# A Strassen sum made by accumulating DMA transfers in place, and the buffer of another sum moved

## The chip, the cores and the metric

One core of one Trainium2 chip. The metric is the device time of one execution in microseconds (us), of the slowest core, which here is the only one.

Names of engines in the profile: PE is TensorE (matmuls), PEld its weight loads, DVE is VectorE, ACT is ScalarE, POOL is GpSimd, SP is SyncE.

## The reference, cut to what matters

```python
# x (8, 4096, 192) -> causal convolution with 7 taps, softmaxed weights per head -> (32768, 192)
h = x @ w_in                        # 192 -> 2048
g = h * np.clip(h + 3, 0, 6) / 6
out = g @ w_out                     # 2048 -> 192, all in float32
```

## The kernel before

The 32768 tokens go through in 32 blocks of 1024. Block 0 is direct; the other 31 use Strassen's scheme with seven products (the variant with sums S1 to S4) for both matrix products. In a block, PE first makes the hidden values (the *hidden phase*, four units of two slots), VectorE gates them into the tile `g`, and then PE makes the output products (the *output phase*). `g` has the quarters A11, A21, A12, A22; the output phase needs

- S1 = A21 + A22, used by product P5,
- S3 = A11 - A21, used by P7,
- S2 = S1 - A11, used by P6, and S4 = A12 - S2, used by P3.

S1 and S3 are made by POOL after every unit, S2 and S4 by VectorE in the output phase. S1 has a buffer of its own, S2, S3 and S4 lie over quarters that are no longer needed.

```python
S2, S3, S4 = A11, A21, A12
...
def h_phase(left):
    for u, plan in enumerate(PLANS):
        ...                                   # matmuls, relu, gates of unit u
        if u:
            g_sums(nc.gpsimd, (1, 3), range(2 * u - 2, 2 * u), 2)
...
forms = {
    1: (S1, A21, A22, ALU.add), 3: (S3, A11, A21, ALU.subtract),
    2: (S2, S1, A11, ALU.subtract), 4: (S4, A12, S2, ALU.subtract),
}
...
def out_strassen(i, conv):
    for u in conv: u()                        # VectorE: convolution of the next block
    b, bank = three(1, 2, 0)                  # PE: P1, a third of P2
    ...
    g_sums(nc.vector, (2,), every, 4)         # VectorE: S2, in two halves
    b, bank = three(4, 2, 1)
    ...
    swap(slice(0, K3))                        # DMA: halves of y change places
    b, bank = by_quarters(2, 2)
    ...
    g_sums(nc.vector, (4,), every, 4)         # VectorE: S4
    b7, bank7 = three(7, 5, 0)                # PE: P7 reads S3, P5 reads S1
    b, bank = three(6, 5, 1)                  # PE: P6 reads S2
    b, bank = three(3, 5, 2)                  # PE: P3 reads S4
```

## Time and profile before

2410.7 us median of 3 runs (2410.63 to 2410.88).

| engine | busy us | share of the span of 2409.1 us |
|---|---|---|
| PE | 2399.2 | 100% |
| DVE | 2088.8 | 87% |
| ACT | 1077.1 | 45% |
| POOL | 671.3 | 28% |
| DMA, 84.65 MB | | 17 to 18% of 16 engines |

How to read it: shares near 100% show candidates for a bound. Only the chain of work that ended last tells whether the others matter, and a block of the timeline tells how much idle time lies between a result and its first use.

### The profile page before, as it was taken

To read this page: it belongs to the slowest core of one execution; us is meant where nothing else is said; L and a number is where in the kernel's file an instruction comes from. 1 tells how busy PE (TensorE), PEld (TensorE's weight loads), DVE (VectorE), ACT (ScalarE), POOL (GpSimd) and SP (SyncE) were. 2 spreads that over 40 slices of the span, in tenths; PEclk is the share of its full clock that TensorE was granted. 3 is DMA by queue.
4 is the path that set the end of the run, shared out by engine and by line. 5 is a ranking of instruction groups with operands and counts; after the bars stand their busy time and mean duration, and the time that the engine had idled before them with its cause. 6 is when DMAs were issued, how large, how long until landed. Compare 5 with 4: busy or idle time off the path is not lost.

```text
span 2409.1 us, 40076 instructions
## 1 busy us (share of the span) xinstructions
PE 2399.2 (100%) x16468; PEld 1008.8 (42%) x16468; DVE 2088.8 (87%) x2534; ACT 1077.1 (45%) x1827; POOL 671.3 (28%) x280
## 2 busy tenths in 40 slices
PE   9999999999999999999999999999999999999998
PEld 4334444334444344443444434444334444344443
DVE  8788888988888888898888898888898888888896
ACT  7234553345543355433454334553335543355433
POOL 2423321233221333122332223322233312333122
PEclk9999999999999999999999999999999999999999
DMA  5211122101122011221112211122201122111210
GB/s 145 40 26 29 27 40 40 39 18 26 39 41 40 19 35 27 40 41 22 32 27 40 41 34 21 27 40 40 40 18 34 30 40 40 21 34 27 40 27 14
DMA packets 227336, 84.65 MB, mean 35 GB/s; under 512 B 205456, under 2 KB 210576, under 8 KB 227152
## 3 DMA queue, kind: packets, MB, share of 16 engines
q1 hardware_dynamic: 225848, 81.56, 17.1%
q8 instruction: 129, 2.11, 0.4%
q10 hardware_dynamic: 1208, 0.27, 0.1%
q14 instruction: 55, 0.45, 0.1%
q0 software_dynamic: 96, 0.26, 0.0%
HBM read 31.72 MB, written 25.17 MB: 24 GB/s over the span
## 4 chain that ended last, share of the span: by engine, by line
PE 99%; DVE 1%; DMA 0%; issue 0%; ACTq 0%; SPq 0%; DVEq 0%
PE psum L311 50%; PE psum L437 48%; DVE y L263 0%; DMA x<-in_x_dram 0%; DMA y<-y 0%; DVE c L541 0%; ACTq L92 0%; DVE scale L174 0%; DVE y L259 0%; DVE sig L199 0%; DVE scale L195 0%; DVE top L178 0%; DVE xt L547 0%; SPq L276 0%; DVEq L259 0%
## 5 line engine op out<-in xcount | busy, mean ns | idle before, releaser
L437 PE MATMUL psum<-g,w_out 128*32 128x512 f32 x9312 | 1163.6, 592 | 0.0
L311 PE MATMUL psum<-y,w_in 64*128 64x512 f32 x3664 | 885.1, 592 | 2.1 <-DVE y L263 1.9
L497 POOL TENSOR_TENSOR s<-g 128x1024 f32<-128x1024 f32 x124 | 293.5, 2367 | 1645.1 <-DVE g L321 1645.1
L317 ACT ACTIVATE r<-psum,half 128x512 f32<-128x512 f32 x1024 | 641.3, 688 | 241.3 <-PE psum L311 234.2
L437 PEld LDWEIGHTS psum<-g,w_out 128*32 128x32 f32 x9312 | 337.4, 110 | 811.7 <-issue 769.9
L321 DVE SCALAR_TENSOR_TENSOR g<-r,psum 128x512 f32<-128x512 f32 x1024 | 641.8, 681 | 4.8 <-ACT r L317 1.1
L437 PE MATMUL psum<-s,w_out 128*32 128x512 f32 x1488 | 638.5, 592 | 0.0
L311 PEld LDWEIGHTS psum<-y,w_in 64*128 64x128 f32 x3664 | 430.2, 187 | 378.7 <-issue 299.4
L311 PE MATMUL psum<-y,w_in_t 64*128 64x512 f32 x1984 | 523.8, 592 | 0.0
L403 DVE TENSOR_TENSOR psum<-psum,p 128x512 f32<-128x512 f32 x496 | 324.6, 694 | 196.0 <-PE psum L311 187.3
L263 DVE SCALAR_TENSOR_TENSOR y<-x,c_sb,y 128x1536 f32<-128x1536 f32 (+1 forms) x210 | 416.6, 1991 | 6.6
L533 ACT COPY c<-psum 32x512 f32<-32x512 f32 x188 | 108.7, 578 | 600.7 <-PE psum L437 599.9
L497 POOL TENSOR_TENSOR g<-g 128x1024 f32<-128x1024 f32 x124 | 338.0, 2725 | 9.7
L311 PEld LDWEIGHTS psum<-y,w_in_t 64*128 64x128 f32 x1984 | 247.1, 186 | 194.3 <-issue 124.9
L541 DVE TENSOR_TENSOR c<-c,psum 32x512 f32<-32x512 f32 (+1 forms) x187 | 128.1, 685 | 81.8 <-ACT c L533 75.8
L396 ACT COPY psum<-psum 128x512 f32<-128x512 f32 x248 | 138.9, 571 | 72.6 <-PE psum L311 57.4
L437 PEld LDWEIGHTS psum<-s,w_out 128*32 128x32 f32 x1488 | 162.4, 110 | 1.2 <-issue 1.2
L399 ACT COPY p<-psum 128x512 f32<-128x512 f32 x248 | 133.2, 591 | 40.7 <-PE psum L311 40.0
L497 DVE TENSOR_TENSOR g<-s,g 128x2048 f32<-128x2048 f32 x62 | 139.3, 2287 | 3.9 <-POOL g L497 2.3
L497 DVE TENSOR_TENSOR g<-g 128x2048 f32<-128x2048 f32 x62 | 139.4, 2289 | 2.0 <-PE psum L437 1.0
L601 ACT COPY c<-psum 96x512 f32<-96x512 f32 x30 | 17.4, 581 | 174.5 <-PE psum L437 174.5
L606 ACT COPY c<-psum 96x512 f32<-96x512 f32 x30 | 17.4, 581 | 170.0 <-PE psum L437 170.0
(46 smaller groups left out, 431.9 us busy)
## 6 DMA issues: line engine op xcount, KB each, us to landing
out_dram<-xt SPq DMA_DIRECT2D x382, 64.0 KB, 2.0
y<-y SPq DMA_DIRECT2D x62, 384.0 KB, 4.8
x<-in_x_dram SPq DMA_DIRECT2D x55, 388.5 KB, 5.7
stage<-in_moe_w_in_dram SPq DMA_DIRECT2D x16, 192.0 KB, 4.4
stage<-in_moe_w_out_dram SPq DMA_DIRECT2D x8, 384.0 KB, 5.2
x<-in_x_dram SPq DMA_DIRECT2D x7, 384.0 KB
y<-y SPq DMA_DIRECT2D x6, 128.0 KB, 2.3
x<-in_x_dram SPq DMA_DIRECT2D x2, 128.0 KB, 4.4
```

The source lines that it names most:

```text
L263: nc.vector.scalar_tensor_tensor(out=to, in0=x[:, part, k + t : k + t + W], scalar=c, in1=to, op0=ALU.mult, op1=ALU.add,)
L311: nc.tensor.matmul(out=psum[:, b], lhsT=w[r], rhs=y[r, third_of_y], start=start, stop=stop, skip_group_check=onto,)
L317: nc.scalar.activation(r6, h, ACT.Relu, bias=half[:], scale=1.0 / 6.0)
L321: nc.vector.scalar_tensor_tensor(out=out, in0=r6, scalar=1.0, in1=h, op0=ALU.min, op1=ALU.mult)
L396: nc.scalar.copy(out=psum[:, bank["b"]], in_=psum[:, bank["a"]])
L399: nc.scalar.copy(out=self.p5[:], in_=psum[:, bank["e"]])
L403: nc.vector.tensor_tensor(out=psum[:, to], in0=psum[:, bank["b"]], in1=self.p5[:], op=ALU.add)
L437: lambda p=p: nc.tensor.matmul(out=bank[j * QS : (j + 1) * QS], lhsT=w_out[:, p, w, cols], rhs=x[:, p], start=(first and p == ps_[0]), sto ...
L497: engine.tensor_tensor(out=o[:, r], in0=a[:, r], in1=b[:, r], op=op)
L533: nc.scalar.copy(out=dst[rows(q)], in_=src[rows(j)])
L541: nc.vector.tensor_tensor(out=out, in0=x, in1=y, op=op)
L601: nc.scalar.copy(out=p1[:], in_=bank[m])
```

## The change

S1 is no longer computed by POOL into a buffer of its own. After each unit, POOL makes S3 alone, into that buffer, and then issues a DMA that adds A22 onto A21 in SBUF; A21 is then S1. The intent is to take about half of the elementwise work off POOL, and with it POOL's collisions with VectorE (in the kernel before, a convolution instruction beside S3 takes 3.81 us where the others take 1.82).

```diff
-    S2, S3, S4 = A11, A21, A12
+    S2, S1, S4 = A11, A21, A12
@@ h_phase
             if u:
-                g_sums(nc.gpsimd, (1, 3), range(2 * u - 2, 2 * u), 2)
+                slots = slice(2 * u - 2, 2 * u)
+                g_sums(nc.gpsimd, (3,), range(NP)[slots], 2)
+
+                nc.gpsimd.dma_start(
+                    out=S1[:, slots], in_=A22[:, slots], accum_op=ALU.add
+                )
@@ g_sums
-            1: (S1, A21, A22, ALU.add), 3: (S3, A11, A21, ALU.subtract),
+            3: (S3, A11, A21, ALU.subtract),
@@ products
-        5: (None, T1), 6: (S2, T2), 7: (S3, T3),
+        5: (S1, T1), 6: (S2, T2), 7: (None, T3),
...
-        return mm(bank, j, S1 if n == 5 else x, w, q, ks, True, True)
+        return mm(bank, j, S3 if n == 7 else x, w, q, ks, True, True)
@@ launch of the blocks
-        S1 = ss.tile([P, NP, N], F32, name="s1")[:]
+        S3 = ss.tile([P, NP, N], F32, name="s3")[:]
```

## The prediction

> **What bounds the kernel now.** I read the page first: the busy table, the slices, the chain of work that ended last. The columns of the first are busy time, share of the span, and instructions.
>
> ```profile
> span 2409.1 us, 40076 instructions
> PE 2399.2 (100%) x16468; PEld 1008.8 (42%) x16468; DVE 2088.8 (87%) x2534; ACT 1077.1 (45%) x1827; POOL 671.3 (28%) x280
> PEclk9999999999999999999999999999999999999999
> PE 99%; DVE 1%; DMA 0%; issue 0%; ACTq 0%; SPq 0%; DVEq 0%
> PE psum L311 50%; PE psum L437 48%; DVE y L263 0%; DMA x<-in_x_dram 0%; DMA y<-y 0%; DVE c L541 0%; ACTq L92 0%; DVE scale L174 0%; DVE y L259 0%; DVE sig L199 0%; DVE scale L195 0%; DVE top L178 0%; DVE xt L547 0%; SPq L276 0%; DVEq L259 0%
> ```
>
> The matmuls are busy for 2399.2 of 2409.1 us at full granted clock, and the chain is PE for 99%. A busy PE could still be a badly pipelined one, so I checked one repeat. The kernel has 31 equal blocks after the first; in the timeline one block runs from 322.96 to 397.22 us, 74.26 us, and has two parts: hidden-layer matmuls (L311, 38.1 us) and output matmuls (L437, 36.2 us). In the steady part of the output phase the timeline starts four quarter-width streams, 8 PE instructions, every 0.86 us, which is 107 ns each; 336 of them make 36.0 of the 36.2 us. No hole is left to win there.
>
> Then the part concerned, the sums of g (L497), by groups:
>
> ```profile
> L497 POOL TENSOR_TENSOR s<-g 128x1024 f32<-128x1024 f32 x124 | 293.5, 2367 | 1645.1 <-DVE g L321 1645.1
> L497 POOL TENSOR_TENSOR g<-g 128x1024 f32<-128x1024 f32 x124 | 338.0, 2725 | 9.7
> L497 DVE TENSOR_TENSOR g<-s,g 128x2048 f32<-128x2048 f32 x62 | 139.3, 2287 | 3.9 <-POOL g L497 2.3
> L263 DVE SCALAR_TENSOR_TENSOR y<-x,c_sb,y 128x1536 f32<-128x1536 f32 (+1 forms) x210 | 416.6, 1991 | 6.6
> ```
>
> The first is S1 on POOL, 124 = 31 blocks x 4 units of two slots. The second is S3, the third S2 on DVE, and the fourth the convolution of the next block, which DVE runs before S2. POOL waits 1645 us in all for the gates, so it is not a bound. Last the order of time in one block; columns are start, duration, engine and what.
>
> ```profile
> 356.37 2.36 POOL L497 TENSOR_TENSOR s<-g 128x1024 f32<-128x1024 f32 x1 [4.64 <-DVE g L321]
> 358.81 2.37 POOL L497 TENSOR_TENSOR g<-g 128x1024 f32<-128x1024 f32 x1
> 362.69 2.40 POOL L497 TENSOR_TENSOR s<-g 128x1024 f32<-128x1024 f32 x1 [1.51 <-DVE g L321]
> 365.17 3.78 POOL L497 TENSOR_TENSOR g<-g 128x1024 f32<-128x1024 f32 x1
> 363.06 1.81 DVE L259 TENSOR_SCALAR y<-x,c_sb 128x1536 f32<-128x1536 f32 x1
> 364.90 13.08 DVE L263 SCALAR_TENSOR_TENSOR y<-x,c_sb,y 128x1536 f32<-128x1536 f32 x6
> 377.89 4.49 DVE L497 TENSOR_TENSOR g<-s,g 128x2048 f32<-128x2048 f32 x2
> 361.04 16.08 PE L437 MATMUL psum<-g,w_out 128*32 128x512 f32 x147
> 376.53 0.59 PE L437 MATMUL psum<-s,w_out 128*32 128x512 f32 x1
> ```
>
> The last S1 is ready at 362.69 + 2.40 = 365.09 us. PE first reads S1 at 376.53, for the last unit three quarters of a 6.86 us group later, at 381.7. DVE starts S2, which reads S1, at 377.89, because it is behind the convolution and not because S1 is late. So the last S1 lies finished for 11 to 17 us. That slack is what the change spends.
>
> [...] The trace before has no accumulating DMA. Its nearest kin is the swap of y, from SBUF to SBUF: 384 KB, 4.8 us to landing; two of them moved 0.79 MB in about 4 us of DMA activity (379 to 383 us), some 200 GB/s[...]. I use the measured rate. [...] in the block shown the first three scalar_tensor_tensor of the convolution average 2482 ns, with S3 beside them, and the next four 1819 ns, with POOL idle; one takes 3.81 us, and S3 stretches from 2.37 to 3.78 us.
>
> **The change part by part.** It removes 124 POOL adds x 2.37 us = 293.5 us of POOL. S3 stays, but is now the first in each unit and writes the separate buffer. It adds 124 DMAs issued from POOL, each adding A22 to A21 over 128 partitions x 1024 f32 = 512 KB. The order of instructions shows that each waits for the S3 before it on POOL (S3 reads A21, which the DMA overwrites). P5 on PE waits for the DMA of each unit separately, S2 on DVE for two at a time.
>
> Duration of one, estimated: a plain copy of 512 KB at 200 GB/s is 2.6 us[...]. On the path: S3 takes the old place of S1, 337.5, 346.9, 356.4 and 362.7, so the DMAs start at 339.8, 349.3, 358.7 and 365.1. They are 9.5, 9.4 and 6.4 us apart, and don't pile up at 4 to 5 us of transfer each. The last lands at 371 to 373 us, before 376.5 and before S2. PE waits for nothing new: 0 us.
>
> Beside the path: DVE loses only the overlap of one POOL add in place of two. In before the loss is 3 x (2482 - 1819) = 2.0 us a block; S3 now ends at 365.1, as the first scalar_tensor_tensor begins (364.9), so nearly all comes back: about 30 x 2.0 = 60 us of DVE, with S2 starting near 376 us. DVE is 87% busy and off the chain, so it buys 0 us of time. The later S3 (3.78 us under contention) falls to 2.4 us. POOL falls from 671 to 671 - 293.5 - 124 x (2.725 - 2.37) = 333 us, the issues not counted.
>
> Buffers: A21 now holds S1, read till the last group of the block (ends at 397.1), where S3 was free one group after 376.5. Its next writers are gates on OTHER results of the next block, from about 330 us in the preceding block's terms, 7 us after the hidden phase began at 323; by then PE has long left the group. A12 holds S4 with the same lifetime already and nobody waits. S3's new buffer is read in one group only, so POOL is free earlier.
>
> Sum: 2410.7 + 0 from PE, with at most some tenths of a microsecond a block for waits that PE now does on DMA semaphores in place of POOL's (the number is the same, four and four). I say 2411.
>
> **The rivals.** (1) The accumulate is slow. If they run one after the other in T us, the last ends at 339.8 + 4T; it must be there by 381.7 us, so T up to 10.5 us (49 GB/s) is hidden. Above it the queue of four bites: T = 11.5 would delay P5 by 4 us a block, 31 x 4 = 124 us, 5%. For it: an addition inside a DMA is nowhere in this trace, and A21 is cut into 2 KB runs where the swap moves 6 KB runs. Against it: the threshold is under half the rate that I estimate. A lone last DMA may even take 16.6 us. (2) VectorE becomes the bound by the chain S2, pieces, S4: S2's second half must start by 390.25 (start of P3) - 2.29 - 2.13 - 2.29 = 383.5 us. That's a later deadline than P5's, so it needs the same slow DMA; 0 us otherwise. (3) The DMAs starve others: DMA share is 0.41 at 330 to 340 us (stores and x) and about 0 from 340 to 376, just where the four run, so they meet little. The swap comes at 378 after the last landing. If the landing slipped to 385, the swap would be slowed by some 3 us, and YS1 has till 397. (4) A gain: freeing POOL and 60 us of DVE might shorten the path. Against it: PE has no hole to fill; at most the 10 us in which PE is not busy, mostly the start that the change doesn't touch, and so never 2%. [...]
>
> **Range and chances.** If the step of zero is right the time moves within about 0.2%, as 31 blocks x 0.1 us is 3 us; that gives 2407 to 2416. I stretch the upper end to 2420 for a delay of 0.3 us a block. Slower by over 2% needs 48 us, 1.6 us a block, which only rival 1 or something unseen in the queue gives: 7%. Faster by over 2%: 1%, since PE alone is busy for 2399 us.
>
> **What would show it.** Right: PE still 2399 us busy and on 99% of the chain; POOL near 333 us; the convolution group down by about 60 us; landing of the new DMAs 6 to 8 us; no wait of PE for a DMA. Wrong: PE weight loads or matmuls that wait for the DMA on g, S2 on DVE idle before it until that DMA, landing above 12 us, or a hidden phase that waits on gates into A21.

The 4 to 5 us of transfer, and with it a landing after 6 to 8 us, are the estimate, above the 2.6 us of a plain copy at the swap's 200 GB/s: no trace before the result showed how long an accumulating DMA takes.

## The result

2410.67 us median of 4 runs (2410.61 to 2410.71), beside 2410.79 us for the kernel before (4 runs). The ratio is 1.0, 95% interval 0.9985 to 1.0014. Ratios here and below are the mean time of one kernel's fast runs over that of the other's of the same rounds, so not quite the ratio of the medians quoted.

The page of the changed kernel: span and busy times, the engines of the chain, four groups of instructions, and one line of the DMA issues (count, size of each, median us from issue to landing).

```profile
span 2408.9 us, 40142 instructions
PE 2399.1 (100%) x16468; PEld 1010.3 (42%) x16468; DVE 2028.6 (84%) x2534; ACT 1077.0 (45%) x1827; POOL 481.5 (20%) x280
...
PE 99%; DVE 1%; DMA 0%; issue 0%; ACTq 0%; DVEq 0%
...
L502 POOL TENSOR_TENSOR s<-g 128x1024 f32<-128x1024 f32 x124 | 292.5, 2359 | 1802.7 <-PE psum L311 1685.4
...
L263 DVE SCALAR_TENSOR_TENSOR y<-x,c_sb,y 128x1536 f32<-128x1536 f32 (+1 forms) x210 | 356.9, 1707 | 6.6
...
L502 DVE TENSOR_TENSOR g<-g 128x2048 f32<-128x2048 f32 x124 | 278.6, 2288 | 5.9 <-DMA g<-g 3.3
...
L431 POOL DMA_DIRECT2D g<-g x124 | 149.1, 1202 | 39.5 <-DVE g L321 27.5
...
g<-g POOLq DMA_DIRECT2D x124, 512.0 KB, 5.0
```

PE is as busy as before to 0.1 us, and still the chain. POOL fell by 189.8 us and VectorE by 60.2 us, 59.7 of it in the convolution (416.6 to 356.9 us), and none of it shows in the span. PE waits for none of the new DMAs; VectorE does so once, for 3.3 us. (In this trace POOL's line puts 1685 us of waiting down to PE, where before it named the gates. POOL's S3 is released by several semaphores, and the last one is inferred; it is the same long wait for the next block's hidden values.)

The timeline of the block that the prediction read, in the changed kernel (start, duration, engine, what):

```profile
362.55 2.38 POOL L502 TENSOR_TENSOR s<-g 128x1024 f32<-128x1024 f32 x1 [2.47 <-issue]
365.23 1.20 POOL L431 DMA_DIRECT2D g<-g  x1 [0.30 <-POOL s L502]
362.92 1.81 DVE L259 TENSOR_SCALAR y<-x,c_sb 128x1536 f32<-128x1536 f32 x1
364.76 11.09 DVE L263 SCALAR_TENSOR_TENSOR y<-x,c_sb,y 128x1536 f32<-128x1536 f32 x6
375.77 4.49 DVE L502 TENSOR_TENSOR g<-g 128x2048 f32<-128x2048 f32 x2
```

The last DMA of the block is issued at 365.23 and lands 5.6 us later, at 370.9; with the median of all 124, 5.0 us, it would be 370.2. The six two-input instructions of the convolution (its *taps*) take 11.09 us in place of 13.08, and S2 starts at 375.77 in place of 377.89. The DMA's activity is seen in windows of 1 us (the last two columns are the mean busy share of the 16 DMA engines, and GB/s moved):

```profile
366.00:367.00 1.00, 1.00 (x16) 0.33 (x12) 0.96 (x2) 0.00 (x0) 0.43 (x1) 1.00 0.09 18
367.00:368.00 1.00, 1.00 (x16) 0.32 (x12) 1.00 (x1) 0.00 (x0) 0.00 (x0) 1.00 1.04 182
368.00:369.00 1.00, 1.00 (x12) 0.26 (x8) 0.96 (x2) 0.93 (x2) 0.00 (x0) 1.00 1.14 193
369.00:370.00 1.00, 1.00 (x16) 0.33 (x12) 1.00 (x1) 0.23 (x1) 0.00 (x0) 1.00 0.84 141
```

The engines are full for about 2.8 us at some 188 GB/s, beginning 1.7 us after the issue.

So the change does what it was meant to do, and it is worth nothing here. The experiments ask four things: whether the buffers or the DMA do what was seen on VectorE; whether PE alone sets the time; how much slack the DMA really has; and what happens beyond it.

### The profile page after: what moved, and what is told of

Same layout as the page of the kernel before. It is cut to its first block, busy times and chain, and to the rows that moved or that the text cites. A ratio compares the mean times of both kernels' runs of the same rounds, so it can differ in the third digit from the quotient of the medians.

```text
span 2408.9 us, 40142 instructions
## 1 busy us (share of the span) xinstructions
PE 2399.1 (100%) x16468; PEld 1010.3 (42%) x16468; DVE 2028.6 (84%) x2534; ACT 1077.0 (45%) x1827; POOL 481.5 (20%) x280
## 4 chain that ended last, share of the span: by engine, by line
PE 99%; DVE 1%; DMA 0%; issue 0%; ACTq 0%; DVEq 0%
PE psum L311 50%; PE psum L442 48%; DVE y L263 0%; DMA x<-in_x_dram 0%; DMA y<-y 0%; DVE c L546 0%; ACTq L92 0%; DVE scale L174 0%; DVE y L259 0%; DVE top L178 0%; DVE sig L199 0%; DVE scale L195 0%; DVE xt L552 0%; DVEq L259 0%; DVEq L552 0%
## 5 line engine op out<-in xcount | busy, mean ns | idle before, releaser
L263 DVE SCALAR_TENSOR_TENSOR y<-x,c_sb,y 128x1536 f32<-128x1536 f32 (+1 forms) x210 | 356.9, 1707 | 6.6
L502 DVE TENSOR_TENSOR g<-g 128x2048 f32<-128x2048 f32 x124 | 278.6, 2288 | 5.9 <-DMA g<-g 3.3
L546 DVE TENSOR_TENSOR c<-c,psum 32x512 f32<-32x512 f32 (+1 forms) x187 | 128.1, 685 | 141.9 <-ACT c L538 136.9
L442 PE MATMUL psum<-s,w_out 128*32 128x512 f32 x1488 | 218.3, 592 | 0.0
L431 POOL DMA_DIRECT2D g<-g x124 | 149.1, 1202 | 39.5 <-DVE g L321 27.5
L442 PEld LDWEIGHTS psum<-s,w_out 128*32 128x32 f32 x1488 | 61.2, 110 | 148.4 <-issue 148.4
L552 DVE STREAM_TRANSPOSE xt<-c 96x512 f32<-96x512 f32 (+1 forms) x125 | 88.1, 704 | 3.3
```

The source lines that it names most:

```text
L263: nc.vector.scalar_tensor_tensor(out=to, in0=x[:, part, k + t : k + t + W], scalar=c, in1=to, op0=ALU.mult, op1=ALU.add,)
L431: nc.gpsimd.dma_start(out=S1[:, slots], in_=A22[:, slots], accum_op=ALU.add)
L442: lambda p=p: nc.tensor.matmul(out=bank[j * QS : (j + 1) * QS], lhsT=w_out[:, p, w, cols], rhs=x[:, p], start=(first and p == ps_[0]), sto ...
L502: engine.tensor_tensor(out=o[:, r], in0=a[:, r], in1=b[:, r], op=op)
L546: nc.vector.tensor_tensor(out=out, in0=x, in1=y, op=op)
```

## The experiments

Eleven kernels, each an edit of the changed one. "Before" ran beside each batch at 2410.74 to 2410.78 us. A deadline is spoken of below: in the block read, PE wants the last unit's S1 at 381.5 us; times of other kernels are shifted to that block by the start of the last S3 (362.55 us). Landings are those of the block shown; the table at the end has the medians of all 31 blocks.

### 1. The buffers alone (e1_inplace_pool)

```diff
-                nc.gpsimd.dma_start(
-                    out=S1[:, slots], in_=A22[:, slots], accum_op=ALU.add
-                )
+                nc.gpsimd.tensor_tensor(
+                    out=S1[:, slots], in0=S1[:, slots], in1=A22[:, slots], op=ALU.add
+                )
```

> The buffer swap alone: POOL itself adds A22 into A21, after S3, and no DMA does it. My theory (all of this lies in slack): 2410.7 us, same, and VectorE back at the kernel of before, that is busy near 2089 us with the convolution group near 416 us, since POOL again has two reading adds a unit; POOL busy 630 to 680 us. Rival (the exchange of the buffers costs something, as A21 now lives to the end of the block, and the DMA hid it): the time moves by more than 2 us.

Measured: 2410.9 us (4 runs), ratio 1.0. Two groups of its page:

```profile
L263 DVE SCALAR_TENSOR_TENSOR y<-x,c_sb,y 128x1536 f32<-128x1536 f32 (+1 forms) x210 | 416.7, 1991 | 6.6
L431 POOL TENSOR_TENSOR g<-g 128x1024 f32<-128x1024 f32 x124 | 338.3, 2728 | 9.7
```

The convolution is back at 416.7 us (before: 416.6), and the second POOL add, now S1, is the one that stretches to a mean of 2728 ns, as S3 did in second place before. The exchange of buffers costs and gains nothing; what VectorE won comes from the add having left POOL.

### 2. A second reading add on POOL, with the DMA kept (e2_pool_read)

```diff
+        scr = ss.tile([P, 2, N], F32, name="scr")[:]
...
                 nc.gpsimd.dma_start(...)
+                nc.gpsimd.tensor_tensor(
+                    out=scr, in0=A22[:, slots], in1=A22[:, slots], op=ALU.add
+                )
```

> The changed kernel with one more POOL add per unit after the DMA is issued, A22 + A22 into a scratch buffer that nobody reads. It brings back POOL's second reading add and leaves the DMA. Theory (VectorE won 60 us because the convolution no longer overlaps a POOL add that reads SBUF): VectorE busy rises by about 60 us to near 2089, S2 starts some 2 us later, and the time stays at 2410.7. Rival (VectorE won because of the new place of S1 or the order): VectorE stays at 2029. If the slack of VectorE were used up, the time would rise by up to 60 us.

Measured: 2410.85 us, ratio 1.0. VectorE rose from 2028.6 to 2075.7 us:

```profile
L263 DVE SCALAR_TENSOR_TENSOR y<-x,c_sb,y 128x1536 f32<-128x1536 f32 (+1 forms) x210 | 403.9, 1930 | 6.6
```

That is 47.0 us more than in the changed kernel and not 60: in the block read the added POOL operation runs from 366.12 to 368.48 us, and the convolution there takes 12.64 us, 1.55 more than 11.09; 30 x 1.55 = 46.5. One tap loses it: it starts at 366.73 us with 1.75 us of the POOL operation left, and takes 3.37 us in place of 1.82. The time did not move: 47 us of VectorE are free either way.

### 3. POOL work that only writes (e3_pool_write)

```diff
                 nc.gpsimd.dma_start(...)
+                for _ in range(3):
+                    nc.gpsimd.memset(scr, 0.0)
```

> As the last, but three POOL fills of a scratch buffer that only write, in place of the add. Theory (it is the reading of two operands on both engines that collides): VectorE stays near 2029 us busy, convolution near 357 us, time 2410.7. Rival (any POOL work collides): VectorE rises by up to 60 us. It also measures the fill, which I need for delays.

Measured: 2411.25 us (2411.14 to 2411.31), ratio 1.0002. The convolution and the fills:

```profile
L263 DVE SCALAR_TENSOR_TENSOR y<-x,c_sb,y 128x1536 f32<-128x1536 f32 (+1 forms) x210 | 372.0, 1778 | 6.6
L435 POOL MEMSET scr<- 128x1024 f32 x372 | 413.7, 1112 | 14.2
```

The convolution lost 15.1 us, where the theory said that it would lose none. In the block read the fills of the unit before push the last S3 to 363.13 us (changed kernel: 362.55), so that it ends at 365.51, 0.65 us after the first two-input tap is due at 364.86. That tap waits and the six take 11.53 us in place of 11.09; 0.44 x 30 = 13 us of the 15. The fills themselves run beside the next taps from 366.55 to 370 us; with the one wait subtracted the six taps have their usual length. So it is reading on both sides that collides here, and writing does not. The 0.5 us of time, outside the spread of the repeats, is not explained; PE is busy for 2399.9 us in its profile.

### 4. Half of a small PE group left out (e5_pe_less)

```diff
-        b, bank = by_quarters(2, 2)
+        b, bank = by_quarters(2, 2, NP // 8)     # half of its matmuls; result wrong on purpose
```

> The changed kernel with half of the matmuls of one small group (P2's last third) left out in 30 blocks; the result is wrong on purpose. 30 blocks x 8 PE instructions x 107 ns = 25.7 us of PE. Theory (PE alone sets the time): 2385 us, within 2. Rival (VectorE at 84% or the sums set it as well): less than 15 us won.

Measured: 2384.86 us (2384.82 to 2385.11), ratio 0.9893, 25.8 us less than the changed kernel's 2410.67. The result is wrong, as intended.

```profile
PE 2373.2 (100%) x16228; PEld 1002.4 (42%) x16228; DVE 2028.0 (85%) x2534; ACT 1076.9 (45%) x1827; POOL 482.6 (20%) x280
```

240 PE instructions fewer, 25.9 us of PE fewer, 25.8 us of time less. Sixty microseconds off VectorE bought nothing, 26 off PE bought 26: PE alone sets the time.

### 5. The last DMA of each block delayed (d8, d12)

```diff
+                if u == UNITS:
+                    for _ in range(8):           # d12: 12
+                        nc.gpsimd.memset(scr, 0.0)
                 nc.gpsimd.dma_start(...)
```

> The changed kernel with eight POOL fills of a scratch buffer between the last S3 of a block and the issue of its DMA: measured at 1.15 us each, so 9.2 us later. The last DMA then lands at 370.2 + 9.2 = 379.4 us of the block I read. My theory of the slack: S2's second half on VectorE, ready to start at 378.1, waits 1.3 us; PE wants P5 of the last unit at 381.5 and waits for nothing; time 2411 us, within 1. Rival (the last DMA is already nearly late): 2411 + up to 31 x 9.2 = 285 us.

> The same with twelve fills, 13.8 us later. The last DMA lands at 384.0: 2.5 us after PE wants it. Theory: PE stands 2.5 us in each of 31 blocks, 78 us, and the granted clock falls after some of the stands as it did with the single large DMA (there 33 us on 110 of standing), so 2490 to 2525 us. Rival (the slack is larger, as PE could work on): 2411. The two runs together bracket the slack at 9.2 to 13.8 us if the theory holds, against 11.3 computed.

A fill behind another took 1.0 us, not 1.15 (the eight took 8.02), so the delays were 7.6 and 11.7 us. Measured: d8 2411.16 us (ratio 1.0002), d12 2541.55 us (2533.37 to 2544.95, ratio 1.0538).

For d8, the issue and S2's second half on VectorE in the timeline:

```profile
372.86 1.20 POOL L434 DMA_DIRECT2D g<-g  x1
...
378.27 2.29 DVE L505 TENSOR_TENSOR g<-g 128x2048 f32<-128x2048 f32 x1 [0.20 <-DMA g<-g]
```

It landed 5.3 us after the issue, 3.4 us ahead of PE's deadline, and VectorE waited 0.2 us. That is as predicted.

d12 is not. With a landing 5.0 us after the issue at 376.9 it would have been 0.4 us late, worth some 12 us in 31 blocks; it cost 131. Its timeline (the block lies 11.26 us later in this kernel):

```profile
388.15 1.20 POOL L434 DMA_DIRECT2D g<-g  x1
...
396.35 2.29 DVE L505 TENSOR_TENSOR g<-g 128x2048 f32<-128x2048 f32 x1 [7.04 <-DMA g<-g]
```

This DMA took 8.1 us to land. The swap of y is issued at 387.17 and 387.72, when the convolution ends, just ahead of it. PE had to stand till 396.3 where it wanted to go on at 392.8, so 3.5 us late in place of 0.4. (Matmuls already started ran on until 393.8, so the profile shows PE idle for 2.5 us of it.)

A second cost stands in windows of 1 us of the same trace (after the length, PE's busy time is the first figure; the clock granted to PE is the third from the end):

```profile
395.00:396.00 1.00, 0.00 (x0) 0.00 (x0) 0.00 (x0) 0.00 (x0) 0.00 (x0) 1.00 0.09 16
396.00:397.00 1.00, 0.72 (x8) 0.38 (x12) 0.65 (x1) 0.00 (x0) 0.00 (x0) 0.86 0.00 0
397.00:398.00 1.00, 1.00 (x8) 0.22 (x4) 1.00 (x1) 0.00 (x0) 0.00 (x0) 0.50 0.00 0
398.00:399.00 1.00, 1.00 (x8) 0.22 (x4) 0.97 (x2) 0.00 (x0) 0.00 (x0) 0.50 0.00 0
```

After PE has stood for 2.5 us its clock is granted at 0.50 for about 3.4 us (the mean from 396 to 401 us is 0.66), and 8 instructions start in a microsecond in place of the 12 to 16 of the windows shown above. It does not follow every gap: 12 of the 31 in d12, whose mean granted clock is 0.991. In the very next block PE is idle for longer, 3.21 us, and keeps the full clock:

```profile
476.50 0.62 PE L445 MATMUL psum<-g,w_out 128*32 128x512 f32 x1 [3.21 <-DMA g<-g]
...
477.00:478.00 1.00, 1.00 (x16) 0.35 (x12) 1.00 (x1) 0.00 (x0) 0.00 (x0) 1.00 0.00 0
```

So the length of a gap alone does not decide. e4_one_dma (experiment 7) shows both as well: a gap of 2.51 us was followed by a mean granted clock of 0.66 over 5 us, one of 2.58 us by 1.00. What does decide was not shown.

The two costs account for d12. In its profiled run PE's weight loads stood 104.3 us for the DMA, and twelve stretches of about 3.4 us at half the clock are worth some 20 us (an estimate: half their length); the run was 128.1 us longer than the changed kernel's.

### 6. Is it the swap? (d11, d12_third_swap)

d11 has eleven fills. The other has twelve, and moves a third of y:

```diff
-        swap(slice(0, K3))
+        swap(slice(0, 1))                        # result wrong on purpose
```

> Eleven fills ahead of the last DMA of a block, that is an issue at about 375.9 us of the block I read, just as the swap of y is issued. With twelve fills (issue at 376.9) the DMA took 8.1 us to land in place of 5.0. Theory A (the swap shares the 16 DMA engines, and a DMA issued with it or after it lands some 2 to 3 us later): it lands at 383 to 384, PE stands 1.5 to 2.5 us a block, time 2460 to 2510 us. Theory B (fixed 5 us to landing, slack 11.3 us): it lands at 381.0, before 381.5, time 2411.

> Twelve fills as before, with only a third of the swap of y transferred (128 KB twice in place of 384 KB twice; the result is wrong on purpose). Theory A (sharing with the swap): the landing falls from 8.1 to about 6 us, PE stands some 1.4 us a block in place of 3.5, time 2440 to 2480 us. Theory C (the fills on POOL themselves make the DMA slow): still 8.1 us and about 2541 us.

Measured: d11 2543.4 us (2542.0 to 2550.42, ratio 1.0556); d12_third_swap 2446.53 us (2445.82 to 2447.26, ratio 1.0149; result wrong). S2's second half on VectorE in d11, where the DMA is issued at 391.69 and the swap at 391.75, and in the other kernel, where the DMA is issued at 378.29:

```profile
401.56 2.29 DVE L505 TENSOR_TENSOR g<-g 128x2048 f32<-128x2048 f32 x1 [7.68 <-DMA g<-g]
```

```profile
383.45 2.29 DVE L505 TENSOR_TENSOR g<-g 128x2048 f32<-128x2048 f32 x1 [3.99 <-DMA g<-g]
```

In d11 the DMA landed 9.7 us after the issue, although it was issued 1 us earlier than in d12; with a third of the swap, at d12's issue time, it landed after 5.0 us. Theory C, that the fills slow it, falls: the fills are the same. Theory A holds, but its size was too small: I expected 2 to 3 us for sharing and d11 shows 4.7. By queue, the packets show waiting as well as sharing. Alone, in the changed kernel, the DMA's first packet came 1.8 us after the issue and its packets took 3.5 us. In d12 the swap's packets ran from 388.3 to 393.0 us and the DMA's only from 391.7 to 396.0, so the first came 3.5 us after the issue. In d11 they ran from 394.8 to 400.9, 6.1 us long, among the swap's from 392.9 to 399.7. Theory B (no stand at all in d11) falls. The 36 us that d12_third_swap still costs are mostly lateness: PE's weight loads stood 31.9 us for the DMA, 1.0 us a block, and no gap (1.6 us at most) was followed by half the clock (the mean granted clock of the run is 1.000).

So the slack is not 11.3 us. A delay of 7.6 us is free, since the DMA still gets ahead of the swap; one of 10.7 us costs 133 us.

### 7. One large DMA a block (e4_one_dma)

```diff
-                nc.gpsimd.dma_start(
-                    out=S1[:, slots], in_=A22[:, slots], accum_op=ALU.add
-                )
+                if u == UNITS:
+                    nc.gpsimd.dma_start(out=S1, in_=A22, accum_op=ALU.add)
```

> One accumulating DMA of all eight slots (2 MB) per block in place of four of 512 KB, issued after the last S3, at 365.2 us of the block I read. At the measured 2.85 us of transfer per 512 KB it takes 11.4 us and some 2.2 us of fixed time, landing at 378.8 or, since the swap of y now runs beside it, up to 380.5. PE needs the first slots at 376.5: theory (slack of the first slots is 11.3 us from issue) 2.3 to 4 us of wait a block, 31 blocks, 2480 to 2535 us. Rival (the slack is far greater, or a large DMA is much quicker): 2411 us. [...]

Measured: 2553.43 us (2553.28 to 2554.03), ratio 1.0592, above the range. Three waits of its trace (total us, times, longest):

```profile
DVE g L501 <- DMA g<-g: 146.0, 31, 16.5
PEld psum L441 <- DMA g<-g: 111.7, 31, 4.9
PE psum L441 <- DMA g<-g: 83.5, 31, 4.0
```

The DMA took 14.6 us to land (median), within the 13.6 to 15.3 that I had worked out (the 2.2 us of fixed time is the changed kernel's 5.0 us to landing less its 2.8 us of transfer), and PE's weight loads stood 111.7 / 31 = 3.6 us a block, inside the 2.3 to 4. The rest, some 31 of the 143 us, goes with the granted clock, whose mean fell from 0.999 to 0.987 (1.2% of 2552 us is 31): an estimate, from the mean of the whole run. POOL took 1.57 us to issue 2 MB and 1.20 us for 512 KB, so the issue grew by no more than 0.37 us.

### 8. More traffic (x2, x3)

```diff
+        scr = ss.tile([P, 2, 2, N], F32, name="scr")[:]     # x3: 3
+        nc.vector.memset(scr, 0.0)
...
+                for e in range(2):                           # x3: 3
+                    nc.gpsimd.dma_start(
+                        out=scr[:, e], in_=A22[:, slots], accum_op=ALU.add
+                    )
                 nc.gpsimd.dma_start(out=S1[:, slots], in_=A22[:, slots], accum_op=ALU.add)
```

> The changed kernel with two more accumulating DMAs of 512 KB per unit, into a scratch buffer, ahead of the real one. At 2.8 us of engine time each one unit takes 8.4 us, under the 9.4 us between units, so no backlog is handed on; the last unit lands near 376, before 381.5. The prediction's rule (hidden up to 10.5 us per unit): 2411 us. Rival (contention of the many DMAs with stores, loads and the swap, or POOL's issues of 1.2 us each, cost time well below that): above 2425.

> Three more per unit: 11.2 us per unit, over the 10.5 of the rule. Four units queue to about 341.5 + 44.8 = 386.3 us and land near 387, and the swap of y at 376 shares the engines: PE stands 5 to 9 us a block, 2565 to 2720 us with some clock lost. Rival (no backlog is formed, or it runs faster): 2411.

Measured: x2 2410.83 us (ratio 1.0001), x3 2818.58 us (2809.16 to 2827.32, ratio 1.1691). Tripling the traffic of the change, to 48.0% of the 16 engines' span on POOL's queue, costs nothing. Quadrupling it costs 408 us:

```profile
PE 2500.5 (89%) x16468; PEld 1017.7 (36%) x16468; DVE 2120.2 (75%) x2535; ACT 1077.4 (38%) x1827; POOL 931.8 (33%) x652
```

PE is idle for 317.5 us of the 2818.0, against 9.8 in the changed kernel, which is 9.9 us a block and a little over the 5 to 9 that I expected; and its matmuls take 101 us more, at a mean granted clock of 0.939. In x3 POOL also stood before several issues until an earlier DMA had landed (203.6 us in all), and the last S3 came late for it. How the excess over the expectation divides into swap, POOL and clock I did not separate. The rule's side of the threshold was right twice: 8.4 us per unit was free and 11.2 was not.

### All runs together

| kernel | median us | last DMA of a block lands after its issue, median of 31 | against PE's deadline, median |
|---|---|---|---|
| changed | 2410.67 | 5.0 us | 11.3 us early |
| d8 | 2411.16 | 5.3 | 3.4 early |
| x2 | 2410.83 | 10.6 | 3.0 early |
| d12_third_swap | 2446.53 | 5.6 | 0.9 late |
| d12 | 2541.55 | 8.1 | 3.5 late |
| d11 | 2543.4 | 9.3 | 3.7 late |

No version beats both kernels. PE has 9.8 us left in which it is not busy, and nothing in this change touches them.

## Why the prediction was right

The step of zero on the path held for the reason it gave. PE was busy 2399.1 us before and after, the chain stayed on it, and the leave-out of 25.7 us of PE came back as 25.8 us of time, which is the direct evidence that a saving elsewhere buys nothing.

The sums beside the path held too. VectorE was to win about 60 us and won 60.2; S2 was to start near 376 and started at 375.77; S3's stretch to 3.78 us was to go and it takes 2.38. POOL was to fall to 333 us with the issues left out; the page counts the new issues as busy, 149.1 us, and 481.5 - 149.1 = 332.4. The cause named for VectorE, one reading POOL operation fewer beside the convolution, is shown by experiments 1 to 3. (The prediction counts seven taps, three slow and four fast; a block has six, of which one was in both of its windows. One alone was stretched, from 1.82 to 3.81 us, so its 2.0 us a block stands.)

One size was off. A new DMA was to land after 6 to 8 us, with 4 to 5 us of transfer; it landed after 5.0 (5.0 to 6.7 over the 124). The transfer took about 2.8 us, some 188 GB/s, close to the 2.6 us of the plain copy at 200 GB/s. What the accumulate adds to a plain copy was the author's estimate, and was mis-sized: by these times it is a factor of about 1.1. By packets it is more: one of 2 KB took 189 ns on average in the changed kernel, and a plain one of 2 KB in the cut swap of d12_third_swap 147 ns, a factor of 1.3. The error was on the safe side.

One argument was incomplete without harm to the forecast. Rival 3 asked what the new DMAs do to the swap, and answered that the swap would be slowed by 3 us and could bear it. It did not ask what the swap does to the last DMA. It also left the swap at 378 us, though it follows the convolution, which was to end 2 us earlier: the swap was issued at 375.92 us in place of 378.04, so the change's own gain on VectorE took 2 us from the distance. Nor did the estimate that a lone last DMA may take 16.6 us: that is the distance to PE's deadline, but beyond some 10 us of delay the DMA falls behind the swap and lands 3 to 5 us later still (8.1 us after the issue in d12, 9.7 in d11, against 5.0). And a missed deadline was counted as the wait alone; the halved clock after it comes on top (in d12 some 20 us, by the estimate above, on 104.3 us of standing). The 5% named for the slow rival was therefore too kind to it: in x3, at 11.2 us per unit where the prediction reckoned with 11.5, the miss cost 17%.

The issues on POOL were even: all 124 took between 1.20 and 1.26 us.

## What to carry to other kernels

Before work is moved off an engine, look at which engine's busy time is the span: here 190 us off POOL and 60 off VectorE bought nothing, and 26 off PE bought 26. When a result is to come from a slower or later source, read its deadline at the consumer, and then see which other transfers start before that deadline, as they may share the DMA engines with it if it slips: here 5.0 us to landing became 8.1 (d12) and 9.7 us (d11) beside the swap. A short stand of PE can cost more than its length: in d12 the granted clock was 0.50 for about 3.4 us after 12 of 31 stands, of 2.5 us on average.
